# Three later passes over 768-token blocks instead of 512, with 384-wide quarter products and the second product two pairs later

## The chip, the cores and the metric

The kernel runs on one core of a Trainium2 chip. A core has TensorE (matrix products, PE in the profile; PEld is its loading of weights), VectorE (DVE), ScalarE (ACT), GpSimd (POOL), and SyncE (SP), which here issues the DMA transfers. Products are collected in PSUM, eight banks of 512 fp32 values on each of 128 partitions; everything else works on SBUF. The metric is device time in microseconds: 870.63 us before the change, the median of three runs from 869.15 to 870.75.

## What is computed

Retention on 4 sequences of 576 tokens with 8 heads of 64 (scores with a decay by distance, no softmax), and on its 2304 x 512 result two feed-forward layers with 2048 hidden features, everything in fp32:

```python
ret = scale * (q @ k.T) * decay          # decay 0 above the diagonal
x = (ret @ v).reshape(2304, 512)
h = x @ w_in                             # 512 -> 2048
x = (h * cos(h)) @ w_out                 # 2048 -> 512
h = x @ w2_in
out = (max(h, 0) + log1p(exp(-abs(h)))) @ w2_out
```

## The kernel before

Every fp32 product of the two layers is made of three products of fp32r parts: each operand is split into a rounded part (names with h) and the rest (names with l), and high by high, high by low and low by high are added. A copy on ScalarE makes the high part, a subtraction on VectorE (or GpSimd) the low part. The weights arrive as 64-bit numbers and are rebuilt by a few bit operations (`convert`, line 335).

The 2048 hidden features are 16 tiles of 128. The work on TensorE is in four passes. The first, `moe_a` (line 996), interleaves the retention with tiles 0 to 7 of the first layer, in five token groups of 512 and 384 with plain products; the half sum goes to DRAM (`pd`). The three later passes are `moe_c` (line 1154), each with four pairs of tiles: `ph` 0 has the rest of layer one, `ph` 1 and 2 the halves of layer two. They go over token blocks of 512, 512, 512, 512 and 256 (`CB`, `CO`), and for each block over the four pairs (`quad`, line 867).

A block of 512 tokens is two halves t of 256; the 512 input features are two halves d, the pair two tiles j. That is a 2 x 2 by 2 x 2 product of quarters, and `quad` makes it with seven products instead of eight (`PRODUCT`, line 864), of combinations of the weight quarters (made once a pass by `weight_pair`, line 434) and of token quarters (made for each block by `x_load_c`, line 1058, which also spills them to DRAM in `ph` 1, so that `ph` 2 only loads them). A product is six matmuls of 256 columns (two of depth 128, three parts each). The four results R1 to R4 come from a chain in PSUM: R1 and R4 lie in one bank, R2 and R3 in another, two pairs of banks (`ha` with `hb`, `s` with `o`) alternate. R1 is copied out (`cv`) after the first and again after the sixth product, R3's first part too (`c5`); VectorE adds these to R2 and R3 (line 932) and R4 = R1 + `c5` (line 935), and the seventh product ("4") is then added to R1. The 256-token block takes plain products, four of them, in one bank.

Then `activate` (line 785) works on each bank of 512: for layer one ScalarE, VectorE, VectorE or ScalarE, ScalarE (sine), VectorE, back into PSUM, for layer two VectorE, ScalarE, VectorE. It ends in the parts gh and gl, in two buffers each (`GB`). The second product takes these within the same pair's time, 24 matmuls of 512 columns: with tokens as columns in layer one, with tokens as weights and the 512 output features as columns in layer two. It is summed over the four pairs in `acc0` to `acc3`, and evicted at a block's end by an addition to the earlier half (`pt`, line 1186) and a store.

What runs when is not written by hand. `Plan` (line 117) takes every operation with an engine, an assumed duration, a due time and its dependences, and in `order` (line 147) puts at each step the operation that can start earliest on its engine, by the due time where two are equal. Constants at the top shift the due times: `XC` how far ahead a block's tokens are asked for, `W2` and `W3` the same for weights, `EARLY` and `EARLY_2` the copies and sums in `quad`. Operations marked "act or dve" or "pool or dve" get their engine there. The instructions are then issued in that order, and each engine runs its own in order.

Of the kernel before, what the change touches and what calls it, by code (L numbers as in the profile page):

```python
# [68 lines left out]
FLEX_AD = 1.075  # L69
FLEX_2 = 50.0  # L70
ROOM = 258.786
SPARE = 0.08
# [8 lines left out]
W2 = (34.03, 6.115, 14.31, 1.214)  # L81
W3 = (31.289, 12.304)
XC = 9.59
# [3 lines left out]
CA = (-3.373, 7.037, 4.372, 2.49)  # L87
TURN = 0.6
XS = 60.0
FILL = (2, 5)  # L90
EARLY = 1.692
EARLY_2 = 8.662
# [5 lines left out]
LL = 0.691  # L98
# [3 lines left out]
LEAD = 7.381  # L102
# [10 lines left out]
KQ = 0.903  # L113
QS = 3
# [136 lines left out]
def retention_moe_moe(ctx, tc, qkv, w1, w2, mask, mtail, dq, dk, out):  # L251
# [8 lines left out]
    xp = pool("xp", 1, side="right")  # L260
    pt = pool("pt", PT, side="right")
    wa_st = [ExitStack(), ExitStack()]
# [14 lines left out]
    sd = [dram.tile([128, len(CB), 7, 512], F32, name=f"sd{g}") for g in "hl"]  # L277
# [3 lines left out]
    mt_t = small.tile([128, 4, 64], F32, name="mt_t")  # L281
    dq_t = cst.tile([128, 4, 320], F32, name="dq_t")
    dk_t = small.tile([128, 12, 1], F32, name="dk_t")
    hp_t = small.tile([128, 1], F32, name="hp_t")
    T = {}
# [31 lines left out]
    UC = lambda n: 42 * t_mm(256) + 24 * t_mm(512) if n == 512 else 24 * t_mm(256) + 12 * t_mm(512)  # L317
    CM, t_ = [], MB
    for order in CO:
        CM.append([t_])  # L320
        for i in order:
            t_ += NP2 // 2 * UC(CB[i][1])
            CM[-1].append(t_)
# [110 lines left out]
    def weight_pair(layer, q, key, step, ahead):  # L434

        slot_ = q % (NP2 // 2)
# [3 lines left out]
        def make():  # L443
            p = wp["qqrp"[slot_]].tile([128, 5632], F32R, tag=f"pair{slot_}", name="pair")
            T[wk] = p[:, 0:1792], p[:, 1792:3584]
            T[wk, "o"] = p[:, 3584:5632].rearrange("p (j g d) -> p j g d", j=2, g=2)

        op("host", 0.0, key, make, r=[("qqrp"[slot_] + "open",)], w=[made], new=[(f"wp{slot_}", 1, wk)])
# [21 lines left out]
        for i, (x, y, o_, r) in enumerate((  # L470
                (lambda: Bv()[:, 0:256], lambda: Bv()[:, 256:512], ALU.add, [ak[1]]),
                (lambda: at(0), lambda: A()[:, 0:256], ALU.subtract, [ak[0], t_(0)]),
                (lambda: A()[:, 0:256], lambda: Bv()[:, 0:256], ALU.subtract, [*ak]),
                (lambda: A()[:, 256:512], lambda: at(1), ALU.subtract, [ak[0], t_(1)]))):
            def combine(e, x=x, y=y, o_=o_, i=i):
                if i % 2 == 0:
                    T[tt[i // 2]] = wp["q"].tile([128, 512], F32, tag="tt", name="tt", bufs=TT)
                e.tensor_tensor(at(i), x(), y(), o_)

            op(POOL_DVE, 256, k + 0.1 * i, combine, r=r + [("qopen",)], w=[t_(i)], new=[] if i % 2 else [("tt", TT, tt[i // 2])])  # L480
        for name, a in (("c", 3), ("d", 5)):
            split(name, a, a + 2, k + 0.6, lambda a=a: T[tt[a // 2 - 1]], [t_(a - 3), t_(a - 2)])
        if ahead:
            oks, ovs = load_values(layer, q, 1, key + 2 * step)
        for j in range(2):
            k = key + (2 + j) * step
            ok, ov = (oks[j], ovs[j]) if ahead else convert(layer, 2 * q + j, 1, k)
            op("act", t_act(512), k + 2.2, lambda j=j, ov=ov: nc.scalar.activation(T[wk, "o"][:, j, 0], ov(), AF.Copy),
               r=[ok, made], w=[(wk, "oh", j)])
            op(POOL_DVE, 512, k + 2.8, lambda e, j=j, ov=ov: sub(e, T[wk, "o"][:, j, 1], ov(), T[wk, "o"][:, j, 0]),  # L490
               r=[ok, (wk, "oh", j)], w=[(wk, "ol", j)])
# [118 lines left out]
    def masks(i, K):  # L610
# [19 lines left out]
        if c:  # L630
            d_k = (("dp", i),)

            def mask_tail():
                st["dp"] = small.tile([128, 64], F32, tag="dp", name="dp", bufs=3)
# [150 lines left out]
    def activate(layer, e, h_k, n, i, K1):  # L785
        kk, rk = ((g, "m", i) for g in ("ek", "er"))
        k_k, r_k = (kk,), (rk,)
        gh_k, gl_k = (("gh", i),), (("gl", i),)
        tmp = lambda g, dt=F32: ew.tile([128, n], dt, tag=g, name=g, padded_shape=[128, 512])
        H_ = lambda: e["h"][:, 0:n]  # L790
        if layer == 1:
# [18 lines left out]
            def a6():  # L810
                nc.vector.tensor_tensor(H_(), H_(), e["r"], ALU.mult)
# [5 lines left out]
            op("dve", t_dve(n), K1 + 2.3, a6, r=[r_k], w=h_k)  # L817
            K2 = K1 + 2.8
        else:
# [7 lines left out]
            def a7():  # L827
                nc.vector.scalar_tensor_tensor(H_(), H_(), 0.0, e["r"], ALU.max, ALU.add)
# [3 lines left out]
            op("dve", t_dve(n), K1 + 1.6, a7, r=[r_k], w=h_k)  # L832
            K2 = K1 + 2.8

        def g1():
            e["gh"] = gp.tile([128, n], F32R, tag="gh", name="gh", padded_shape=[128, 512])
            nc.scalar.activation(e["gh"], H_(), AF.Copy)

        def g2():
            e["gl"] = gp.tile([128, n], F32R, tag="gl", name="gl", padded_shape=[128, 512])  # L840
            sub(nc.vector, e["gl"], H_(), e["gh"])

        op("act", t_act(n, True), K2, g1, r=h_k, w=[gh_k], new=[("gh", GB, gh_k[0])])
        op("dve", t_dve(n), K2 + 0.5, g2, r=h_k + [gh_k], w=[gl_k], new=[("gl", GB, gl_k[0])])
# [20 lines left out]
    GROUP = "aabccdd"  # L865

    def quad(layer, q, xk, n, K, u, acc_id, acc, first, last):

        i = slots[0]
        slots[0] += 2
        wk = ("wp", layer, q)
        whole = n == 512
        tag_a, tag_b = (("ha", "hb"), ("s", "o"))[i // 2 % 2] if whole else (HT[i // 2 % 4], None)
        ka, kb = (tag_a, "q", i), (tag_b, "q", i)
        r1, r4, r2, r3 = (kb, 1), (kb, 4), (ka, 2), (ka, 3)
        ea, eb = {}, {}

        def banks():
            ea["h"] = bank(tag_a)
            eb["h"] = bank(tag_b) if whole else ea["h"]

        R1, R4 = (lambda z=z: eb["h"][:, z * 256:z * 256 + 256] for z in range(2))
        R2, R3 = (lambda z=z: ea["h"][:, z * 256:z * 256 + 256] for z in range(2))

        def product(out_, wi, xi, start, stop=True):
            y = 0
            for c in range(2):  # L890
                w_ = lambda g: T[wk][g][:, wi * 256 + c * 128:wi * 256 + c * 128 + 128]
                x_ = lambda g: T[xk][g][:, xi, c * 256:c * 256 + 256]
                for a, b in ((0, 0), (0, 1), (1, 0)):
                    nc.tensor.matmul(out_, w_(a), x_(b), start=(start and y == 0), stop=(stop and y == 5), skip_group_check=True)  # L894
                    y += 1

        def pe(todo, k, w, new=()):

            def run():
                if new:  # L900
                    banks()
                for o_, wi, xi, st in todo:
                    product(o_(), wi, xi, st)

            wi = sorted({GROUP[t[1]] for t in todo})
            op("pe", 6 * len(todo) * t_mm(256), k, run,
               r=[(wk, g, z) for g in "hl" for z in wi] + [(xk, g, t[2]) for g in "hl" for t in todo], w=w, new=list(new))

        new = [(tag_a, 1, ka), (tag_b, 1, kb)] if whole else [(tag_a, 1, ka)]
        if whole:  # L910
            P = lambda o_, z, st: (o_, *PRODUCT[z], st)
            ck, c5k = ("cv", i), ("c5", i)
            pe([P(R1, 1, True), P(R2, 2, True), P(R3, 5, True)], K, [r1, r2, r3], new)
            e = {}

            def copy_1(eng):
                e["cv"] = wp["q"].tile([128, 512], F32, tag="cv", name="cv", bufs=2)
                copy(eng, e["cv"][:, 0:256], R1())

            def copy_5(eng):  # L920
                e["c5"] = wp["q"].tile([128, 256], F32, tag="c5", name="c5", bufs=2)
                copy(eng, e["c5"], R3())

            def copy_6(eng):
                copy(eng, e["cv"][:, 256:512], R1())

            op(ACT_DVE, (t_act(256, True), t_dve(256)), K + 0.7 - EARLY, copy_1, r=[r1, ("qopen",)], w=[(ck, 0)], new=[("cv", 2, ck)])
            op(ACT_DVE, (t_act(256, True), t_dve(256)), K + 2.1 - EARLY, copy_5, r=[r3, ("qopen",)], w=[(c5k,)], new=[("c5", 2, c5k)])
            pe([P(R1, 6, False)], K + 0.9, [r1])
            pe([P(R3, 3, False)], K + 1.5, [r3])  # L930
            op(ACT_DVE, (t_act(256, True), t_dve(256)), K + 4.0 - EARLY, copy_6, r=[r1], w=[(ck, 1)])
            op("dve", t_dve(512), K + 4.5 - EARLY_2, lambda: nc.vector.tensor_tensor(ea["h"], ea["h"], e["cv"], ALU.add),
               r=[(ck, 0), (ck, 1)], w=[r2, r3])
            pe([P(R1, 7, False)], K + 2.0, [r1])
            op("dve", t_dve(256), K + 5.5 - EARLY, lambda: nc.vector.tensor_tensor(R4(), R1(), e["c5"], ALU.add), r=[r1, (c5k,)], w=[r4])  # L935
            pe([P(R1, 4, False)], K + 3.0, [r1])
        else:
            pe([(R2, 0, 0, True), (R2, 1, 1, False)], K, [r2], new)
            pe([(R3, 3, 0, True), (R3, 2, 2, False)], K + 1.0, [r3])
            both = activate(layer, ea, [r2, r3], 512, i, K + 0.5 * u)  # L940
        late = 0.0 if whole else LAG_S * u
        for j, (e_, hk, ready) in enumerate(((ea, [r2, r3], 0.45 * u), (eb, [r1, r4], 0.75 * u))):
# [332 lines left out]
```

## Time and profile before

| | |
|---|---|
| runs | 870.75, 870.63, 869.15 us, median 870.63 |
| the profiled execution: span | 871.2 us; no other time of it is given |
| TensorE busy | 857.9 us (98%), 5780 matmul instructions |
| weight loads busy | 753.3 us (86%) |
| VectorE busy | 647.2 us (74%) |
| ScalarE busy | 452.6 us (52%) |
| GpSimd busy | 47.3 us (5%), none after 300 us |
| DMA | 160.11 MB, mean 184 GB/s |
| chain that ended last | TensorE 92%, VectorE 3%, ScalarE, DMA and issue 1% each |

The span runs from the first to the last instruction of the profiled execution. Matmuls overlap in the array, so the listed duration of one (0.28 us for 256 columns, 0.39 for 512) is longer than the step from one to the next; the step is what a stream of them costs, and it is read from the chain of waits or from the starts in the timeline. The first quarter product (line 894) starts at 283.9 us; from there on the three later passes fill the rest.

### The profile page before, as it was taken

The numbers are of one execution on the slowest core, as the hardware profiler recorded it, in microseconds if no ns is written. First come the engines' busy times: TensorE is split into PE (matmuls) and PEld (weight loads), VectorE is DVE, ScalarE is ACT, GpSimd is POOL, SyncE is SP. The second block draws the span as 40 slices with busy tenths as digits, with TensorE's granted clock in tenths as the row PEclk, the third lists the DMA queues.
The fourth block names the chain that finished last, engine by engine and source line by source line (L and its number), as shares of the span: only waits on it lengthen the run. The fifth ranks groups of instructions, "written<-read, shape, count | busy, mean of one in ns | idle before, by whom it ended". The sixth has DMA issues, their size and how long they took to land.

```text
span 871.2 us, 15110 instructions
## 1 busy us (share of the span) xinstructions
PE 857.9 (98%) x5780; PEld 753.3 (86%) x5780; DVE 647.2 (74%) x1227; ACT 452.6 (52%) x873; POOL 47.3 (5%) x66
## 2 busy tenths in 40 slices
PE   7989999999999999999999999999999999999998
PEld 5768777899987889899898888998889888888897
DVE  3779987877479997578589997888568756465643
ACT  1368765756456855445458765655255533232221
POOL 3620100100030000000000000000000000000000
PEclk9989999999999999999999999999999999999999
DMA  9876779775363803245338469777525442432203
GB/s 312 319 267 187 275 250 340 259 271 173 131 229 97 254 22 101 64 144 166 110 117 283 146 252 316 225 252 311 217 92 190 165 170 97 169 97 73 97 2 108
DMA packets 67432, 160.11 MB, mean 184 GB/s; under 512 B 6048, under 2 KB 25632, under 8 KB 65312
## 3 DMA queue, kind: packets, MB, share of 16 engines
q1 hardware_dynamic: 67360, 159.15, 52.8%
q8 instruction: 45, 0.74, 0.4%
q14 instruction: 27, 0.22, 0.1%
HBM read 104.08 MB, written 55.05 MB: 183 GB/s over the span
## 4 chain that ended last, share of the span: by engine, by line
PE 92%; DVE 3%; ACT 1%; DMA 1%; issue 1%; SPq 0%; POOL 0%; DVEq 0%; POOLq 0%; ACTq 0%
PE acc L959 34%; PE acc L858 10%; PE o L894 9%; PE hb L894 9%; PE ha L894 7%; PE s L894 7%; PE ha L758 5%; PE hb L758 4%; PE o L671 2%; PE s L594 1%; PE o L758 1%; PE s L758 1%; PE s L599 1%; DMA dq_t<-in_dq 1%; DMA raw<-in_qkv 1%
## 5 line engine op out<-in xcount | busy, mean ns | idle before, releaser
L959 PE MATMUL acc<-pair,gh 128*128 128x512 f32 x576 | 179.3, 392 | 0.0
L959 PEld LDWEIGHTS acc<-pair,gh 128*128 128x128 f32 x576 | 101.3, 189 | 14.9
L959 PE MATMUL acc<-pair,gl 128*128 128x512 f32 x288 | 112.3, 390 | 0.0
L959 PE MATMUL acc<-gh,pair 128*128 128x512 f32 (+1 forms) x320 | 99.7, 370 | 0.0
L825 ACT ACTIVATE er<-er 128x512 f32<-128x512 f32 x72 | 45.5, 632 | 91.4 <-DVE er L822 91.4
L894 PE MATMUL o<-x,pair 128*128 128x256 f32 x328 | 78.3, 284 | 0.7 <-ACT cv L303 0.7
L894 PE MATMUL hb<-x,pair 128*128 128x256 f32 x328 | 78.8, 285 | 0.0
L894 PE MATMUL hb<-xx,pair 128*128 128x256 f32 x320 | 77.9, 285 | 0.0
L894 PE MATMUL o<-xx,pair 128*128 128x256 f32 x320 | 77.6, 285 | 0.0
L959 PEld LDWEIGHTS acc<-gh,pair 128*128 128x128 f32 x320 | 58.5, 189 | 8.6
L959 PEld LDWEIGHTS acc<-pair,gl 128*128 128x128 f32 x288 | 54.1, 188 | 11.8
L894 PEld LDWEIGHTS o<-x,pair 128*128 128x128 f32 x328 | 57.7, 189 | 5.1 <-DVE o L935 1.6
L894 PEld LDWEIGHTS hb<-x,pair 128*128 128x128 f32 x328 | 57.8, 189 | 4.9 <-DVE hb L935 2.4
L894 PEld LDWEIGHTS hb<-xx,pair 128*128 128x128 f32 x320 | 56.7, 189 | 5.0 <-DVE hb L935 2.1
L894 PEld LDWEIGHTS o<-xx,pair 128*128 128x128 f32 x320 | 56.6, 189 | 4.4 <-DVE o L935 2.1
L858 PE MATMUL acc<-gl,wh 128*128 128x512 f32 (+1 forms) x160 | 59.2, 370 | 1.2 <-DVE gl L299 1.2
L858 PE MATMUL acc<-gh,wh 128*128 128x512 f32 (+1 forms) x160 | 60.3, 377 | 0.0
L959 PE MATMUL acc<-gl,pair 128*128 128x512 f32 (+1 forms) x160 | 59.3, 371 | 0.0
L858 PE MATMUL acc<-gh,wl 128*128 128x512 f32 (+1 forms) x160 | 58.9, 368 | 0.0
L894 PE MATMUL ha<-x,pair 128*128 128x256 f32 x256 | 58.5, 283 | 0.0
L894 PE MATMUL s<-x,pair 128*128 128x256 f32 x256 | 58.5, 283 | 0.0
L808 ACT ACTIVATE er<-er,hp_t 128x512 f32<-128x512 f32 (+1 forms) x76 | 52.9, 697 | 10.5 <-DVE er L805 9.5
(196 smaller groups left out, 1999.8 us busy)
## 6 DMA issues: line engine op xcount, KB each, us to landing
wr<-in_w SPq DMA_DIRECT2D x64, 512.0 KB, 4.3
wd<-wk SPq DMA_DIRECT2D x40, 256.0 KB, 3.9
wr<-wd SPq DMA_DIRECT2D x20, 512.0 KB, 3.9
raw<-in_qkv SPq DMA_DIRECT2D x12, 640.0 KB, 5.4
raw<-in_qkv SPq DMA_DIRECT2D x12, 512.0 KB, 5.7
od<-pt SPq DMA_DIRECT2D x18, 256.0 KB, 2.4
pt<-od SPq DMA_DIRECT2D x18, 256.0 KB, 2.8
out<-pt SPq DMA_DIRECT2D x18, 256.0 KB, 2.0
```

Of the source, the lines that this page charges most:

```text
L594: nc.tensor.matmul(X()[j][:, z], k_(j, z), q_(z)[Z[j]], start=True, stop=True)
L599: nc.tensor.matmul(X()[0][Z[j], at_u(z)], kt_()[:, z, j], st["v"]()[:, z, j], start=True, stop=True)
L671: nc.tensor.matmul(o_at(z)[Z[j]], lhs(j), rhs(j), start=start, stop=stop, skip_group_check=True)
L758: nc.tensor.matmul(h_[:, 0:n], lhs, rhs[:, d, 0:n], start=(k == 0), stop=(k == 3 * NC - 1))
L808: nc.scalar.activation(e["r"], e["r"], AF.Sin, bias=hp_t[:, 0:1], scale=-1.0)
L825: nc.scalar.activation(e["r"], e["r"], AF.Softplus)
L858: nc.tensor.matmul(acc[o][:, 0:n], l[:, s], e[r], start=(first and z == 0), stop=(last and z == 2))
L894: nc.tensor.matmul(out_, w_(a), x_(b), start=(start and y == 0), stop=(stop and y == 5), skip_group_check=True)
L959: nc.tensor.matmul(acc[m][:, 0:n] if layer == 1 else acc[m], l, r, start=(begin and z == 0), stop=(stop and z == 2))
```

## The change

`CB` becomes three blocks of 768 tokens. A half block is 384 tokens, and all blocks take the seven products, now of 384 columns (`HN`). R1 to R4 have a bank each (`ha`, `hb`, `s`, `o`), so there is one set of four and not two of two. `activate` writes its last step to SBUF (`g`, three or four buffers for each half and tile), which frees the bank; gh and gl are made from there, still in two buffers, when the second product is due. That product is cut into units: `unit` does one half block t for one pair s, due in the time of pair 2 + 2t + s // 2, thus two pairs or more later and partly in the next block. Per unit there are 24 matmuls of 384 in `ph` 0, 18 of 512 in the others; the four `acc` banks hold one half block at a time. The token quarters lie in nine slots used in turn, so that the next block's can come while the last are in use. Weights for the second product have a tile of their own (`weight_out`). The jobs are given to the planner in order of due time, and its constants have new values. The first pass keeps its code; its last group's second products are due later (`LL`).

```diff
-CB = ((0, 512), (512, 512), (1024, 512), (1536, 512), (2048, 256))
-CO = ((0, 1, 4, 2, 3), (0, 1, 4, 2, 3), (0, 1, 2, 3, 4))
+HN = 384
+CB = tuple(range(0, NT, 2 * HN))
+NS = 9
...
-FLEX_AD = 1.075
+FLEX_AD = 0.993
-XC = 9.59
+XC = 9.717
-LL = 0.691
+LL = 3.862
+LAG = -2.133
+LEAD_G = 7.197
+GT = (3, 4)
...
+    DT = 6 * t_mm(HN)
+    IN, OUT = 7 * DT, (24 * t_mm(HN), 18 * t_mm(512))
+    UC = [IN + 2 * OUT[ph > 0] for ph in range(3)]
+    KI = lambda ph, y, s: CM[ph] + (half_p * y + s) * UC[ph]
...
-                nc.vector.scalar_tensor_tensor(H_(), H_(), 0.0, e["r"], ALU.max, ALU.add)
+                nc.vector.scalar_tensor_tensor(dst() if dst else H_(), H_(), 0.0, e["r"], ALU.max, ALU.add)
...
+    def quad(ph, y, s):
...
+        product(1, 1, K, True, True)
+        op(ACT_DVE, both, K + DT - EARLY, keep(1, 0, "v"), r=[rk[1], ("qopen",)], w=[(cv, 0)], new=[("cv", 2, cv)])
+        product(2, 2, K + DT, True, True)
+        product(3, 5, K + 2 * DT, True, True)
+        op("dve", t_dve(HN), K + 3 * DT - EARLY_2, lambda: nc.vector.tensor_tensor(R(2), R(2), c["v"][:, 0], ALU.add), r=[(cv, 0)], w=[rk[2]])
+        op(ACT_DVE, both, K + 3 * DT - EARLY, keep(3, 0, "5"), r=[rk[3], ("qopen",)], w=[(c5,)], new=[("c5", 2, c5)])
+        product(1, 6, K + 3 * DT)
+        op(ACT_DVE, both, K + 4 * DT - EARLY, keep(1, 1, "v"), r=[rk[1]], w=[(cv, 1)])
+        product(3, 3, K + 4 * DT)
+        product(1, 7, K + 5 * DT)
...
+        op("dve", t_dve(HN), K + 6 * DT - EARLY, fourth, r=[rk[1], (c5,)], w=[rk[4]], new=free(4))
+        op("dve", t_dve(HN), K + 5 * DT - EARLY_2, lambda: nc.vector.tensor_tensor(R(3), R(3), c["v"][:, 1], ALU.add), r=[(cv, 1)], w=[rk[3]])
+        product(1, 4, K + 6 * DT)
+        for r, j, t, ready in ((2, 0, 0, 3), (3, 0, 1, 6), (4, 1, 1, 6.5), (1, 1, 0, 7)):
...
+                    T[gk] = wp["r"].tile([128, HN], F32, tag=f"g{t}{j}", name="g", bufs=GT[t])
...
+    def unit(ph, y, t, s):
...
+        K = KI(ph, y, 2 + 2 * t + s // 2) + IN + (s % 2) * OUT[ph > 0] - LAG
...
+        for j in range(2):
...
+            Kj = K + j * OUT[ph > 0] / 2
+            rd = parts(e, lambda gk=gk: T[gk], [(gk,)], HN, i, Kj - LEAD_G, False)
+            for m in range(nm):
...
+                op("pe", OUT[ph > 0] / (2 * nm), Kj + 0.01 * m, mo, r=rd + [(wk, g, j) for g in "hl"], w=[(ak,)],
+                   new=[(tag, 1, ak)] if first else [])
...
+    XHOME = "qqqqrrrpp"
...
+            n = uses[0] % NS
+            uses[0] += 1
```

On TensorE, in the last pass, the end of one pair's quarter products before: hb holds R1 and R4, ha R2 and R3, x and xx are the token quarters' parts, pair the weights; the first piece is the product added before R4 is taken, the last six are the product behind it.

```order
L894 MATMUL hb<-x,pair 128x256
L894 MATMUL hb<-xx,pair 128x256
L894 MATMUL hb<-x,pair 128x256 x2
L894 MATMUL hb<-xx,pair 128x256
L894 MATMUL hb<-x,pair 128x256
L959 MATMUL acc_6495<-pair,gh 128x512 x2
L959 MATMUL acc_6495<-pair,gl 128x512
L894 MATMUL hb<-x,pair 128x256
L894 MATMUL hb<-xx,pair 128x256
L894 MATMUL hb<-x,pair 128x256 x2
L894 MATMUL hb<-xx,pair 128x256
L894 MATMUL hb<-x,pair 128x256
```

And now, where ha is R1, hb R2, s R3:

```order
L921 MATMUL hb<-x,pair 128x384 x6
L921 MATMUL s<-x,pair 128x384 x6
L921 MATMUL ha<-x,pair 128x384 x6
L921 MATMUL s<-x,pair 128x384 x6
L921 MATMUL ha<-x,pair 128x384 x6
L1001 MATMUL acc_6956<-pair,gh 128x512 x2
L1001 MATMUL acc_6956<-pair,gl 128x512
L1001 MATMUL acc_6963<-pair,gh 128x512 x2
L1001 MATMUL acc_6963<-pair,gl 128x512
L921 MATMUL ha<-x,pair 128x384 x6
L1001 MATMUL acc_6980<-pair,gh 128x512 x2
L1001 MATMUL acc_6980<-pair,gl 128x512
```

Six 512-wide matmuls of the second product stand now before the last product of a pair where three stood, and between the products on s, and on ha before, there are six of 384 where there were six of 256.

On VectorE, in the second pass, the making of gl among a block's preparation before: x and xx are token quarters (512 wide), tt their combinations, er and ha or hb the activation.

```order
L828 SCALAR_TENSOR_TENSOR hb<-hb,er 128x512
L371 SCALAR_TENSOR_TENSOR wk<-wy,wk 128x512
L299 TENSOR_TENSOR gl<-ha,gh 128x512
L299 TENSOR_TENSOR pair<-wr,pair 128x512
L299 TENSOR_TENSOR gl<-hb,gh 128x512
L299 TENSOR_TENSOR xx<-tt,x 128x512 x3
L1094 TENSOR_TENSOR tt<-xx,tt 128x512
L299 TENSOR_TENSOR xx<-xx,x 128x512
L932 TENSOR_TENSOR s<-s,cv 128x512
L935 TENSOR_TENSOR o<-o,c_5766 128x256
```

And now, with x and tt 768 wide and g the activated values in SBUF:

```order
L308 TENSOR_TENSOR x<-tt,x 128x768
L848 SCALAR_TENSOR_TENSOR g<-s,er 128x384
L308 TENSOR_TENSOR gl<-g,gh 128x384
L848 SCALAR_TENSOR_TENSOR g<-o,er 128x384
L308 TENSOR_TENSOR x<-tt,x 128x768
L308 TENSOR_TENSOR gl<-g,gh 128x384
L842 TENSOR_SCALAR er<-ha 128x384
L308 TENSOR_TENSOR x<-x 128x768
L848 SCALAR_TENSOR_TENSOR g<-ha,er 128x384
L308 TENSOR_TENSOR x<-tt,x 128x768
L308 TENSOR_TENSOR gl<-g,gh 128x384
L1175 TENSOR_TENSOR tt<-x,tt 128x768
```

The subtractions that make gl stood in pairs, one a half pair; now there are twice as many, each 384 wide, and single splits or combinations of 768 stand between them.

## Rows read from the trace of the kernel before

**Rows 1.** The page's first part: busy us, share of span, instructions.

```profile
PE 857.9 (98%) x5780; PEld 753.3 (86%) x5780; DVE 647.2 (74%) x1227; ACT 452.6 (52%) x873; POOL 47.3 (5%) x66
```

**Rows 2.** Busy time by stretch: stretch, length, each engine, TensorE clock, DMA share, GB/s.

```profile
283.90:478.00 194.10, 193.40 (x1258) 176.10 (x1257) 157.29 (x282) 116.38 (x217) 0.00 (x0) 1.00 0.43 139
478.00:672.00 194.00, 194.00 (x1215) 174.11 (x1214) 156.93 (x277) 108.86 (x208) 0.00 (x0) 1.00 0.62 220
672.00:867.10 195.10, 195.10 (x1204) 173.53 (x1202) 111.81 (x188) 61.33 (x115) 0.00 (x0) 1.00 0.31 114
867.10:871.20 4.10, 0.15 (x1) 0.00 (x0) 0.95 (x3) 0.00 (x0) 0.00 (x0) 0.78 0.35 128
```

**Rows 3.** Chain of waits, one pair of the last pass: start, us, what.

```profile
...
605.70 0.71 PE hb L894 x6
606.41 1.44 PE ha L894 x12
607.85 0.69 PE acc L959 x3
608.54 0.71 PE hb L894 x6
609.25 0.72 PE ha L894 x6
609.97 0.73 PE hb L894 x6
610.71 0.70 PE acc L959 x3
611.40 0.81 PE hb L894 x6
612.21 4.11 PE acc L959 x18
...
```

**Rows 4.** Chain of waits in the first pass, 384 and 512 wide.

```profile
...
185.79 2.08 PE ha L758 x12
...
265.01 2.72 PE ha L758 x12
...
```

**Rows 5.** Timeline within that pair: start, us, engine, line, operation, idle before it.

```profile
...
609.09 0.28 PE L894 MATMUL ha<-x,pair 128*128 128x256 f32 x1
609.29 0.38 ACT L303 ACTIVATE cv<-hb 128x256 f32<-128x256 f32 x1 [2.46 <-PE hb L894]
...
609.81 0.30 PE L894 MATMUL hb<-x,pair 128*128 128x256 f32 x1
...
610.42 0.28 PE L894 MATMUL hb<-x,pair 128*128 128x256 f32 x1
...
610.74 0.43 DVE L935 TENSOR_TENSOR hb<-hb,c 128x256 f32<-128x256 f32 x1
...
611.24 0.38 PE L894 MATMUL hb<-x,pair 128*128 128x256 f32 x1
611.45 0.28 PE L894 MATMUL hb<-xx,pair 128*128 128x256 f32 x1
...
```

**Rows 6.** Line 894: what its engine sat idle for (us, times).

```profile
...
  DVE hb L935: 4.5, 17
  DVE o L935: 3.8, 15
...
```

**Rows 7.** Groups by shape on VectorE and ScalarE: busy us, mean ns, idle before.

```profile
...
L299 DVE TENSOR_TENSOR gl<-hb,gh 128x384 fp32r<-128x384 f32 x6 | 3.3, 554 | 2.2 <-ACT gh L837 2.1
...
L303 ACT ACTIVATE pt<-acc 128x384 f32<-128x384 f32 x8 | 3.7, 493 | 0.1
L802 ACT ACTIVATE er<-er 128x384 f32<-128x384 f32 x6 | 3.1, 519 | 0.7 <-DVE er L798 0.6
...
```

**Rows 8.** Waits of TensorE from 200 to 300 us: total, times, longest.

```profile
...
PE acc L858 <- DVE gl L299: 0.6, 2, 0.5
```

**Rows 9.** The page's last part, DMA issues: KB each, us to landing.

```profile
...
wr<-wd SPq DMA_DIRECT2D x20, 512.0 KB, 3.9
...
```

More of the change, by code (lines that the diff above doesn't have):

```diff
@@ L284, in retention_moe_moe @@
     hp_t = small.tile([128, 1], F32, name="hp_t")
+    small.tile([128, PAD], F32, name="pad")
     T = {}
@@ L865, in retention_moe_moe @@
     GROUP = "aabccdd"
-    def quad(layer, q, xk, n, K, u, acc_id, acc, first, last):
+    xof = lambda ph, y, i: ("xc", ph, y, i)
+    gof = lambda ph, y, s, t, j: ("g", ph, y, s, t, j)
+    def quad(ph, y, s):
+        layer = 2 if ph else 1
+        q = s if ph == 1 else half_p + s
+        K = KI(ph, y, s)
         i = slots[0]
-        slots[0] += 2
+        slots[0] += 4
         wk = ("wp", layer, q)
[L875 to L897, printed above, removed]
@@ L899, in run, with product @@
+        tag = dict(zip((1, 2, 3, 4), HT))
+        key = {r: (tag[r], "q", i) for r in tag}
+        rk = {r: (key[r],) for r in tag}
+        e = {r: {} for r in tag}
+        R = lambda r: e[r]["h"][:, 0:HN]
+        cv, c5 = ("cv", i), ("c5", i)
+        free = lambda r: [(tag[r], 1, key[r])]
+        def product(r, z, k, start=False, new=False):
+            w_i, x_i = PRODUCT[z]
             def run():
                 if new:
-                    banks()
-                for o_, wi, xi, st in todo:
-                    product(o_(), wi, xi, st)
@@ L905, in pe @@
[L905 to L913, printed above, removed]
-            e = {}
[L916 to L940, printed above, removed]
@@ L941, in quad @@
[L941 to L955 removed]
+                    e[r]["h"] = bank(tag[r])
@@ new lines, in run @@
+                n = 0
+                for c in range(2):
+                    w_ = lambda g: T[wk][g][:, w_i * 256 + c * 128:w_i * 256 + c * 128 + 128]
+                    x_ = lambda g: T[xof(ph, y, x_i)][:, g, c * HN:c * HN + HN]
+                    for a, b in ((0, 0), (0, 1), (1, 0)):
+                        nc.tensor.matmul(R(r), w_(a), x_(b), start=(start and n == 0), stop=(n == 5), skip_group_check=True)
+                        n += 1
+            op("pe", DT, k, run, r=[(wk, g, GROUP[w_i]) for g in "hl"] + [(xof(ph, y, x_i), g) for g in "hl"], w=[rk[r]],
+               new=free(r) if new else [])
@@ new lines, in quad, with keep, run @@
+        both = (t_act(HN, True), t_dve(HN))
+        c = {}
+        def keep(r, z, name):
+            def run(eng):
+                if name == "5":
+                    c["5"] = wp["q"].tile([128, HN], F32, tag="c5", name="c5", bufs=2)
+                elif z == 0:
+                    c["v"] = wp["q"].tile([128, 2, HN], F32, tag="cv", name="cv", bufs=2)
+                copy(eng, c["5"] if name == "5" else c["v"][:, z], R(r))
+            return run
+        product(1, 1, K, True, True)
+        op(ACT_DVE, both, K + DT - EARLY, keep(1, 0, "v"), r=[rk[1], ("qopen",)], w=[(cv, 0)], new=[("cv", 2, cv)])
@@ L956, in mo @@
                     else:
[L957 removed]
+                        prods = [(l[:, z_], e[r]) for l, r in ((hi, "gh"), (hi, "gl"), (lo, "gh"))]
                     for z, (l, r) in enumerate(prods):
[L959 to L962 removed]
+                        nc.tensor.matmul(acc[m] if ph else acc[m][:, 0:HN], l, r, start=(first and z == 0), stop=(last and z == 2))
```

372 lines of the change are left out of this document (201 added, 171 removed).

## Prediction, made before the changed kernel was run

> **What bounds the kernel now.** I read the busy shares first: TensorE is busy for 857.9 us of the 871.2 us of the profiled span [rows 1]. The profiled execution has no time of its own apart from that span; the span is 0.6 us over the median of the timed runs (870.63 us), so I work on the span and take 0.6 us off at the end. Then the busy times by stretch. The change touches the three later passes, and these are the stretch from the first quarter product at 283.9 us to the last matmul at 867.1 us: 583.2 us, TensorE busy in practically all of it, at the full granted clock (2.4 GHz). VectorE is busy for 81% of the first two thirds (157.3 of 194.1 us and 156.9 of 194.0) and 57% of the last [rows 2]. So TensorE's stream sets the time, and VectorE is the engine to watch.
>
> Then the chain of waits, for the price of that stream. In an undisturbed part of the last pass one pair of hidden tiles on 512 tokens is nine pieces: 0.71, 1.44, 0.69, 0.71, 0.72, 0.73, 0.70, 0.81 and 4.11 us, 10.62 us in all [rows 3]. Twelve 256-wide matmuls take 1.44 us, 0.120 each; eighteen 512-wide ones 4.11 us, 0.2283 each. The 384-wide form is already in the first pass: twelve take 2.08 us, 0.1733 each, beside 2.72 us (0.2267) for 512 in the same code [rows 4]. From 256 to 512 a column costs 0.107/256 = 0.00042 us, so each matmul carries about 0.0133 us whatever its width; 384 lies on that line (0.1600 + 0.0133).
>
> Does it close? A pass has 4 blocks of 512 (16 pairs at 10.62 = 169.9 us) and one of 256 with plain products. The small block's pair is 24 matmuls of 256 and 12 of 512 in passes two and three (2.88 + 2.74 = 5.62, times 4 = 22.5), and 48 of 256 in pass one (5.76, times 4 = 23.0). That is 192.9 + 192.4 + 192.4 = 577.7 us, and with 24 matmuls that the first pass still has to do there (5.4 us) 583.1, against 583.2 measured. What the pieces are made of is thus all that there is, and no block start or pass start costs more than tenths.
>
> **The change part by part.** *Widths and counts.* Three blocks of 768, all with seven products, twelve pairs a pass. A pair has 42 matmuls of 384 (7.28 us) and a second product of 48 matmuls of 384 in pass one (8.32 us), 36 of 512 in the others (36 x 0.2283 = 8.22). Passes: 12 x 15.60 = 187.2 and twice 12 x 15.50 = 186.0; sum 559.2. Against 577.7 that is 18.5 us less. It has two sources. Matmuls alone: 2400 of 256 and 1248 of 512 become 2088 of 384 and 864 of 512, at the prices above 13.2 us less; 9,216 columns are 3.8 of it (the 256 block gets the saved product too) and 696 fixed parts of 0.0133 are 9.3. The other 5.3 us are waits inside the old pair, the next item.
>
> *The waits inside a pair.* In rows 3 the last six-matmul piece takes 0.81 us where its like take 0.71, and the one before 0.73. Rows 5 show why: the last product of a pair needs VectorE's sum, VectorE starts 0.20 us after the product before has been issued (610.54 to 610.74), takes 0.43, and TensorE goes on normally from 611.45, 0.09 us late; only three 512-wide matmuls (0.70 us) stand between. The copy by ScalarE goes the same way: its product has been issued at 609.09, where the next piece starts, the copy runs from 609.29 to 609.67, and the piece that waits for it starts at 609.81 with a first matmul 0.02 too long; 0.72 us stand between. All matmuls of that line show 8.3 us of idle time that the sums ended, 32 times, in the weight loads [rows 6]; most of that is hidden behind matmuls that still run. I take 0.11 us a pair, 48 pairs, 5.3 us.
>
> After the change the copies and sums are 384 wide: ScalarE 0.493, VectorE 0.554 us [rows 7]. With the same hand-overs (0.20 before, 0.16 behind) a copy needs 0.85 us and a sum 0.91. By the order, six 384-wide matmuls (1.04 us) or more stand between in every one of the 36 quads, and in passes two and three six 512-wide ones (1.37 us) before the last product. So these waits should go, by 0.13 to 0.46 us of slack, wherever the engine is free.
>
> *What is late next.* The activated values wait in SBUF, so the second product no longer hangs on the activation chain. But its operands gh and gl are made just before use, in two buffers, and one set now serves only 12 matmuls of 384 (2.08 us) or 9 of 512 (2.05 us) instead of 12 of 512 (2.74). A buffer's turn is: hand-over 0.20, ScalarE 0.52 (SBUF to SBUF [rows 7]), about 0.06, VectorE 0.554, hand-over 0.16; 1.5 us, an estimate from these rows. That leaves 0.5 us for whatever stands in front in VectorE's or ScalarE's queue. An operation of 384 just fits, one of 768 on VectorE does not: from 0.43 us for 256 [rows 5] and 0.554 for 384 I estimate 0.93 for it, so that the set would come 0.37 us late. The trace shows no such wait in the passes, since the old buffers had 2.74 us; bounds are 0 and, if each of the 96 sets of passes one and two met one operation of 768, 0.37 x 96 = 36 us. The nearest row is the old pair itself, which lost 0.11 us; I take 0.11 for each of the 36 new pairs, 4.0 us, and keep both ends.
>
> *VectorE and ScalarE in sum.* 144 activations of 384 take the place of 108 of 512, on the same columns. The 36 more are about three VectorE operations each with a fixed part of 0.18 us (0.554 less three steps of 0.124), 20 us; by the order 35 copies of 256 leave VectorE for ScalarE, 15 us. A few us over three passes, and at 81% that is covered by TensorE's stream: nothing in itself.
>
> *Rest of the edits.* Spilled operands are the same bytes in more transfers, asked for about 10 us ahead as before: nothing, hidden by the block before; if that cover failed, one landing of 3.9 us [rows 9] at each of 9 block starts, 35 us. Weights of the second product get their own slot and come later; their last use and next use lie two pairs (31 us) apart: nothing. The first pass ends with its second products later, so that two waits for gl (0.6 us [rows 8]) can go: -0.6. The tail is the same: two half-width sums of the last tile and its store behind the last matmul, 4.1 us [rows 2].
>
> Sum: 871.2 - 18.5 + 4.0 - 0.6 = 856.1 on the span, 855.5 as a run's time.
>
> **A rule against it.** The rows give each matmul 0.0133 us beside its columns [rows 3, 4]. The Trainium skill ("TensorE: Matmul & The Clock Gate", section "Back-to-back issue gap") gives a single matmul N/2.4 + 2.5 ns, which makes the fixed part five times smaller; by it the 696 matmuls fewer would be worth 1.7 us and not 9.3. The trace disagrees at all three widths (120, 173 and 227 ns, not 109, 163 and 216), so the sum goes by the rows; by the rule the time would be 1.7 us under that of the first rival.
>
> **Rivals.** *The fixed part stays.* If what I read as a cost of each matmul were a cost of each product or of the splits, only the columns (3.8), the balance of waits (5.3 - 4.0) and the 0.6 would be gained: 871.2 - 5.7 - 0.6 = 864.9 us. For it: the 256 rows and the 512 rows are different code. Against: 384 and 512 in one code lie on the same line. Chance 0.04.
>
> *Part is given back.* The buffers of gh and gl wait now and then: 0.05 to 0.1 us for each of 144 sets, 7 to 14 us in place of the 4.0: 858.7 to 865.7, middle 862. For it: VectorE's busy 81%, and the order, in which splits of 768 stand between two gl. Against: the slack of 0.5 us. Chance 0.25.
>
> *Slower.* The same place, but as a rule and not now and then: in passes one and two VectorE's queue is so mixed that each set comes late by 0.25 us, 96 x 0.25 = 24 us: 855.5 - 4.0 + 24 = 875.5. It decides from 19.1/96 = 0.20 us a set on. For it: each wait delays the activations behind it in the queue, which free the four product banks. Against: the old passes ran on that same share of VectorE, and their pieces close to 0.1 us without room for such waits. Chance 0.08.
>
> **Numbers.** My forecast has 0.63, with a range of its own of 851 (no new waits: 855.5 - 4.0 = 851.5) to 859. The range of 0.8: 850.5 to 864, which ends just under the first rival and takes in the given-back case but for its top. A measurement tells about 0.2% (1.7 us) from no change. Of the slower case's 0.08 I put 0.07 beyond that and 0.01 within it; 0.02 more within is a given-back case that goes further than priced. The rest, 0.90, is faster.
>
> **What would show it.** After: 2088 matmuls of 384 outside the first pass; a pair in the last pass of about 15.5 us in the chain, with no six-matmul piece longer than 1.06; passes of 186 to 190 us; and, in the list of waits, TensorE's on gl and gh of the second product below 5 us. The forecast is wrong if twelve 384-wide matmuls take over 2.1 us there, or if TensorE idles by more than 10 us between the first quarter product and the end; the window with the lowest TensorE share then says in which pass.

## The result, and the profile after

The changed kernel takes 858.48 us (median of 4 runs, 857.71 to 859.36) against 870.69 us for the kernel before (median of 4). The two medians give a ratio of 0.9860; the ratio on record is 0.9852, interval 0.9832 to 0.9873. In a second set of runs it was 0.9841 (0.9823 to 0.9859). The forecast of 855.5 us is 3 us low, inside its range and at the top of its own narrower one (851 to 859); the gain is 12 to 14 us where 15 were forecast.

The page of the changed kernel, busy time by engine and the chain by engine; it answers to [rows 1]:

```profile
PE 842.1 (98%) x5084; PEld 756.9 (88%) x5084; DVE 653.2 (76%) x1281; ACT 480.0 (56%) x951; POOL 53.2 (6%) x73
PE 86%; DVE 7%; ACT 3%; issue 1%; DMA 1%; SPq 0%; POOL 0%; DVEq 0%; POOLq 0%; ACTq 0%
```

TensorE has the 696 matmuls fewer and is as full as before. New is VectorE in the chain: 7% where it was 3%. Of its 63 us there 47 lie in the first pass and 14 in the first 80 us of the later passes; behind that the chain is TensorE's.

Its busy time by stretch, with columns as in [rows 2]; the first stretch begins at the first quarter product, the last is the tail:

```profile
278.06:470.00 191.94, 189.94 (x1074) 185.97 (x1073) 166.21 (x316) 133.03 (x261) 0.00 (x0) 1.00 0.41 139
470.00:661.00 191.00, 191.00 (x974) 174.65 (x973) 153.33 (x288) 111.63 (x215) 0.00 (x0) 1.00 0.61 218
661.00:851.90 190.90, 190.90 (x944) 170.75 (x942) 110.27 (x205) 70.58 (x142) 0.00 (x0) 1.00 0.33 114
851.90:855.90 4.00, 0.21 (x1) 0.00 (x0) 1.01 (x3) 0.00 (x0) 0.00 (x0) 0.78 0.53 197
```

Only the first stretch has idle time on TensorE (2.0 us). From the first quarter product to the last matmul there are 573.9 us; 36 matmuls of 512 belong to the first pass (36 x 0.2267 = 8.2), so the three passes take 565.7. The same reckoning on [rows 2] gives 583.2 - 5.4 = 577.8. The passes gained 12.1 us. A second execution of each kernel gives the same lengths: 565.7 and 577.8.

The chain of waits, one pair of the last pass (start, us, what); it answers to [rows 3]:

```profile
696.44 1.06 PE hb L921 x6
697.50 1.04 PE s L921 x6
698.54 1.04 PE ha L921 x6
699.58 1.04 PE s L921 x6
700.62 1.04 PE ha L921 x6
701.66 1.39 PE acc L1001 x6
703.05 1.04 PE ha L921 x6
704.10 4.80 PE acc L1001 x21
708.90 1.06 PE ha L921 x6
709.96 2.08 PE acc L1001 x9
```

A pair is 15.60 us (the next begins at 712.04); 15.61 was forecast (15.50 and 0.11). No wait is left in it. What is over the bare prices (42 x 0.1733 + 36 x 0.2267 = 15.44) lies where the width changes: the 512 pieces take 1.39, 4.80 and 2.08 us, not 1.36, 4.76 and 2.04, and two pieces of 384 behind them 1.06 and not 1.04. By the starts of the single matmuls it is up to 12 ns in each of the first five to nine behind a change.

Waits of TensorE in the passes (total, times, longest):

```profile
PE acc L1001 <- DVE gl L308: 1.1, 2, 0.8
PE s L921 <- DVE gl L308: 0.9, 1, 0.9
```

Both lie in pass one. The chain there (start, us, what):

```profile
279.88 0.70 DVE o L831
280.58 0.60 DVE gl L308
281.18 0.04 issue
281.23 1.33 PE s L921 x6
...
340.94 0.46 DVE pt L1034
341.40 0.48 DVE gl L308
341.87 0.04 issue
341.92 1.15 PE acc L1001 x5
...
```

At 281.23 the third quarter product has waited for bank s, which a gl of the first pass's last group was made from (VectorE works on the PSUM banks too, and ScalarE reads them): with one set of four banks the first quad needs all of them at once. At 341.92 the second product waits for gl behind the evictions (pt) at the start of the second block.

Groups by shape on VectorE, which answer to [rows 7] (busy us, mean ns, idle before):

```profile
L308 DVE TENSOR_TENSOR gl<-g,gh 128x384 fp32r<-128x384 f32 x144 | 79.6, 554 | 66.6 <-ACT gh L862 66.0
...
L308 DVE TENSOR_TENSOR x<-tt,x 128x768 fp32r<-128x768 f32 x24 | 22.7, 951 | 0.2 <-ACT x L1182 0.2
```

A 384-wide operation takes the 0.554 us assumed, a 768-wide one 0.951 (estimated at 0.93).

### The profile page after: what moved, and what is told of

It reads as the page before. It is cut to its first block, busy times and chain, and to the rows that moved or that the text cites. A ratio compares the mean times of both kernels' runs of the same rounds, so it can differ in the third digit from the quotient of the medians.

```text
span 855.9 us, 13829 instructions
## 1 busy us (share of the span) xinstructions
PE 842.1 (98%) x5084; PEld 756.9 (88%) x5084; DVE 653.2 (76%) x1281; ACT 480.0 (56%) x951; POOL 53.2 (6%) x73
## 4 chain that ended last, share of the span: by engine, by line
PE 86%; DVE 7%; ACT 3%; issue 1%; DMA 1%; SPq 0%; POOL 0%; DVEq 0%; POOLq 0%; ACTq 0%
PE acc L1001 34%; PE ha L921 17%; PE acc L883 9%; PE s L921 8%; PE hb L921 4%; PE ha L779 4%; PE hb L779 3%; PE o L692 2%; PE s L615 1%; DVE tt L1175 1%; DVE wk L382 1%; PE s L779 1%; PE s L620 1%; DMA dq_t<-in_dq 1%; DVE gl L308 1%
## 5 line engine op out<-in xcount | busy, mean ns | idle before, releaser
L921 PE MATMUL ha<-x,pair 128*128 128x384 f32 x864 | 174.3, 336 | 0.0
L921 PEld LDWEIGHTS ha<-x,pair 128*128 128x128 f32 x864 | 152.6, 188 | 5.1 <-DVE g L831 0.3
L308 DVE TENSOR_TENSOR gl<-g,gh 128x384 fp32r<-128x384 f32 x144 | 79.6, 554 | 66.6 <-ACT gh L862 66.0
L862 ACT ACTIVATE gh<-g 128x384 fp32r<-128x384 f32 x144 | 74.8, 521 | 92.1 <-PE acc L1001 88.4
L1001 PE MATMUL acc<-gh,pair 128*128 128x384 f32 x384 | 105.1, 334 | 0.0
L845 ACT ACTIVATE er<-er 128x384 f32<-128x384 f32 x96 | 50.3, 524 | 73.5 <-DVE er L842 73.0
L921 PE MATMUL s<-x,pair 128*128 128x384 f32 x432 | 86.8, 335 | 0.9 <-DVE gl L308 0.9
L921 PEld LDWEIGHTS s<-x,pair 128*128 128x128 f32 x432 | 75.9, 188 | 1.5 <-DVE gl L308 1.2
L1001 PE MATMUL acc<-gl,pair 128*128 128x384 f32 x192 | 64.5, 336 | 1.1 <-DVE gl L308 1.1
L828 ACT ACTIVATE er<-er,hp_t 128x384 f32<-128x384 f32 (+1 forms) x88 | 56.3, 643 | 15.5 <-DVE er L825 14.2
```

The source lines that it names most:

```text
L308: e.tensor_tensor(out_, a, hi.bitcast(F32), ALU.subtract)
L828: nc.scalar.activation(e["r"], e["r"], AF.Sin, bias=hp_t[:, 0:1], scale=-1.0)
L845: nc.scalar.activation(e["r"], e["r"], AF.Softplus)
L862: nc.scalar.activation(e["gh"], src(), AF.Copy)
L921: nc.tensor.matmul(R(r), w_(a), x_(b), start=(start and n == 0), stop=(n == 5), skip_group_check=True)
L1001: nc.tensor.matmul(acc[m] if ph else acc[m][:, 0:HN], l, r, start=(first and z == 0), stop=(last and z == 2))
```

## The experiments

Edits are against the changed kernel, unless the text says before. To compare with the changed kernel I set ratios beside its two, 0.9852 and 0.9841.

**The two kernels again.** Both unchanged.

> The kernel before once more, for its profile. If the part of the first pass ahead of 53 us (retention, TensorE waiting 2.9 us and then at the lower clock) differs between executions by chance, the first quarter product starts up to 2 us earlier than at 283.9 us here, and the span is nearer to the runs' median than 871.2. If the 3.1 us by which the first pass is shorter in the changed kernel come from the changed constants, it starts at 283.9 us again within 0.5.

> The changed kernel once more, on the chip of the other runs of this set, as what they are compared with: 858.5 us within 1, ratio to the kernel before 0.985. Pairs of passes two and three 15.60 us again.

The kernel before gave 872.77 us, with a span of 870.9; the changed kernel 858.25 us (857.54 to 859.41), spans 855.8 to 857.6. A run is thus 1.8 us longer than its span. Most of what differs between executions is the first pass: counted to the end of its matmuls, 289.3 and 289.1 us before, 286.2 and 287.9 after, and both kernels have code for it that differs little. The expectation's sign for the constants was seen: in the kernel before the first quarter product starts at 283.6 us, within 0.5 of 283.9. But in the changed kernel it starts at 279.7 us in this execution and at 278.1 in the first, with no constant changed. The granted clock of these executions shows much of why. First the kernel before, then the changed kernel, 20 to 60 us (the third column from the right is the clock):

```profile
20.00:40.00 20.00, 20.00 (x322) 15.40 (x321) 14.04 (x50) 6.49 (x20) 12.10 (x19) 0.93 0.95 365
40.00:60.00 20.00, 17.06 (x187) 13.63 (x184) 15.66 (x46) 11.06 (x31) 7.01 (x9) 0.83 0.74 255
```

```profile
20.00:40.00 20.00, 20.00 (x348) 15.55 (x342) 15.68 (x53) 5.97 (x19) 12.23 (x20) 1.00 0.93 368
40.00:60.00 20.00, 17.12 (x193) 13.42 (x189) 17.22 (x47) 14.36 (x36) 7.78 (x10) 0.91 0.82 273
```

The second execution of each, in the same order:

```profile
20.00:40.00 20.00, 20.00 (x316) 15.56 (x312) 13.74 (x49) 6.13 (x20) 12.11 (x20) 0.91 0.98 364
40.00:60.00 20.00, 17.02 (x200) 13.45 (x200) 17.04 (x49) 12.12 (x32) 7.36 (x9) 0.91 0.70 257
```

```profile
20.00:40.00 20.00, 20.00 (x316) 15.40 (x312) 13.62 (x49) 5.76 (x19) 12.09 (x20) 0.91 0.96 362
40.00:60.00 20.00, 17.48 (x206) 13.85 (x204) 17.09 (x49) 12.87 (x34) 7.80 (x10) 0.91 0.77 263
```

The means of 0.93, 0.83 and 0.91 are stretches at 1.2 GHz within 2.4, after TensorE had paused or been half idle (2.5 us without a matmul before 48.5 us in the changed kernel). Between the first two executions that is 20 x 0.07 + 20 x 0.08 = 3.0 us, against 3.1 between their first passes, and between the two of the changed kernel 1.8 against 1.7. But between the two of the kernel before it is 1.2 against 0.2, and between the second two nothing against 1.2, so this reckoning is good to about 1 us. Of the 15.3 us between the two profiled spans 12.1 are the change's passes, 0.1 the tail and 3.1 the first pass, most of that the clock; what the change itself takes from the first pass is 0.1 us by one pair of executions and 1.2 by the other. The medians (12.2 and 13.8 us apart) carry the 12.1 and at most 1.7 of first pass.

**More room before the last product, in the kernel before.** The planner is told that the sum for R4 takes 0.2 us longer, which puts six matmuls of 512 and not three ahead of a pair's last product.

```diff
-op("dve", t_dve(256), K + 5.5 - EARLY, lambda: ... R4() ...
+op("dve", t_dve(256) + 0.2, K + 5.5 - EARLY, lambda: ... R4() ...
```

> The kernel before, with the planner told that VectorE's sum for R4 takes 0.2 us longer, so that six 512-wide matmuls and not three stand ahead of a pair's last product. If the 0.10 us there are a wait for that sum, the pieces of 0.81 us become 0.72, a pair 10.52 us, and the run is about 4.6 us shorter (866.1). If they are only the cost of going from 512 to 256 columns, nothing changes (870.7). The order changes elsewhere too, by up to 1 us either way.

869.39 us, ratio 0.9965 (0.9952 to 0.9979), 3.1 us less. The chain in the last pass, where [rows 3] had 0.70, 0.81 and 4.11:

```profile
...
607.27 0.73 PE hb L894 x6
608.01 1.39 PE acc L959 x6
609.40 0.71 PE hb L894 x6
610.11 3.43 PE acc L959 x15
...
```

The piece of 0.81 is back at 0.71. It stood there in 33 of the old pairs (over 0.77 us; 33 x 0.10 = 3.3 us over their like), not in all 48, and stands in 3 here. So the mechanism is shown, and the old waits were worth about 3 us, not 5.3. In this version the passes are 2.3 us shorter, although a new wait at 445 us costs about 0.4.

**What a matmul costs beside its columns.** In pass three each quarter matmul is cut into 256 and 128 columns.

```diff
-nc.tensor.matmul(R(r), w_(a), x_(b), ...)
+for u, v in ((0, 256), (256, 384)):
+    nc.tensor.matmul(R(r)[:, u:v], w_(a), x_(b)[:, u:v], ...)
```

> The changed kernel with each 384-wide matmul of the quarter products of the last pass cut into one of 256 and one of 128 columns: 504 matmuls more, the same columns. If each matmul carries 0.0133 us beside its columns, a pair of that pass goes from 15.60 to 16.16 us and the run is 6.7 us longer (865.2). If a matmul carries 0.0025 us, 1.3 us longer (859.8). If the fixed part belongs to a product or to a switch between products, no change (858.5).

888.06 us, ratio 1.0179 (1.0161 to 1.0198): 29 us more, over four times what was expected. One pair of the last pass:

```profile
...
704.43 1.34 PE hb L923 x12
705.76 1.38 PE s L923 x12
707.15 1.39 PE ha L923 x12
...
```

Six of 256 and six of 128 take 1.34 to 1.39 us where six of 384 took 1.04. By the line through 256, 384 and 512 it would be 6 x (0.120 + 0.067) = 1.12 us. The starts show where the rest goes: a matmul of 128 is followed by the next one after 0.057 to 0.062 us, but one of 256 mostly only after 0.17, not 0.120. Every matmul here loads weights of its own, and the loads start one behind another, every 0.108 to 0.126 us, in this pass never closer than 0.108; two of them fill the 0.224 to 0.232 us of a 256 and a 128. There is a floor under the two matmuls together, so this run says nothing on the fixed part. The next expectation reads 0.111 us for 128 columns from the chain, which the starts don't bear out. The Trainium skill ("TensorE: Matmul & The Clock Gate", section "LDWEIGHTS (loading the stationary operand)") puts such a load at its columns over 1.2 in ns, 107 for 128; the 0.108 agrees with it. No run here took the load away, so that the load is the floor is read from these starts and was not tried.

So the second product of pass three was cut instead, each 512 into two of 256, above the floor.

```diff
-nc.tensor.matmul(acc[m] ..., l, r, ...)
+for u in (0, 256):
+    nc.tensor.matmul(acc[m][:, u:u + 256], l, r[:, u:u + 256], ...)
```

> The changed kernel with each 512-wide matmul of the second product of the last pass cut into two of 256, a width that the kernel before uses throughout: 432 matmuls more, the same columns. The cut to 128 columns before fell under a floor (0.111 us for 128 columns, read from its chain), which says nothing of wider ones. If each matmul of 256 or more carries 0.0133 us beside its columns, the run is 432 x 0.0133 = 5.7 us longer (864.0). If 256 columns, too, stand on a floor of the weight load and the parts of 0.0133 belong to something else, anything from 0 to 2.

863.26 us, ratio 0.9893 (0.9876 to 0.9909), 3.6 to 4.5 us over the changed kernel; its passes take 4.0 us more. The chain, parts of a pair:

```profile
...
752.67 1.04 PE ha L921 x6
753.71 5.03 PE acc L1003 x42
758.74 1.04 PE ha L921 x6
759.78 2.15 PE acc L1003 x18
...
```

A pair is 15.90 us: bare prices 42 x 0.1733 + 72 x 0.120 = 15.92. The 36 matmuls more cost 0.48 (0.0133 each), and the 0.16 for changes of width are gone: beside 256 the 384 pieces all take 1.04. Both together are the 0.30 seen. The fixed part of 0.0133 us holds. By the 2.5 ns that the Trainium skill ("TensorE: Matmul & The Clock Gate", section "Back-to-back issue gap") gives a single matmul beside its columns, 36 more would by estimate cost 0.09 us, less than the 0.16 that goes, and the pair would have become shorter.

**Three buffers for gh and gl.** `GB` 3; to have the room, `cv` and `c5` get one buffer each.

```diff
-GB = 2
+GB = 3
...
```

> The changed kernel with three buffers for gh and gl instead of two; to make room the kept copies cv and c5 have one buffer instead of two. If the waits on gl at the second block of pass one (about 335 and 341 us, 1.4 us in all) come from the turn of two buffers, they go, and the run is 1 to 2 us shorter (857). If they come from VectorE's order there, they stay, and nothing changes (858.3 within 0.7). Passes two and three stay at 15.60 us a pair under both.

859.18 us, ratio 0.9851 (0.9833 to 0.9868), the passes 565.6 us: nothing. TensorE's waits in the passes:

```profile
PE ha L921 <- ACT cv L312: 1.9, 1, 1.9
PE acc L1001 <- DVE gl L308: 0.8, 1, 0.8
```

The wait for gl at the second block stays, so it isn't for a buffer. The wait for `cv` took the place of the one for bank s; it is for the first copy of all, so no buffer was missing. The timeline shows what stood in front of that copy on ScalarE, while in the changed kernel the planner has the copy on VectorE:

```profile
...
282.04 2.29 ACT L1182 ACTIVATE x<-tt 128x768 fp32r<-128x768 f32 x3
...
284.24 0.47 ACT L312 ACTIVATE cv<-ha 128x384 f32<-128x384 f32 x1
...
```

The two gh and gl buffers are not what the passes lost to.

**The planner's constants.** `XC` asks for a block's tokens earlier, `LL` puts the first pass's last second products where they were before, `LAG` moves the units of the second product.

```diff
-XC = 9.717
+XC = 13.0
```

> The changed kernel with the tokens of each block asked for 13.0 us ahead and not 9.7. If the 1.07 us that TensorE loses at the third quarter product of pass one (281 us) are the preparation of the token quarters coming late on VectorE, the run is about 1 us shorter (857.3); the waits on gl at the second block may go or grow by as much. If they are the transfer, it also goes. Otherwise no change.

863.19 us, ratio 0.9898 (0.988 to 0.9915), some 4.5 us slower, against the expectation. The passes are 568.5 us, 2.8 more; in the first pass there is a new wait of 1.6 us for gl at 267 us. New in the passes are waits for copies:

```profile
PE ha L921 <- ACT cv L312: 1.8, 2, 1.2
PE s L921 <- ACT c L312: 1.3, 2, 0.7
```

At the first of them (283.8 us) splits of 768 stand ahead of the copy on ScalarE. That this holds for the others is how I read it; it was not tried by itself.

```diff
-LL = 3.862
+LL = 0.691
```

> The changed kernel with the last group of the first pass as before (LL 0.691). If the shorter first pass of the changed kernel's profile (3.1 us less than in the profile of before) came from that edit by the waits on gl that it took away, the run is 0.6 to 1 us longer (859); if it is mostly TensorE's clock around 40 to 60 us, which differs between executions, no more than that; if the edit made all of it, 3 us longer (861.3).

866.19 us, ratio 0.9932 (0.9918 to 0.9946), 7 to 8 us slower than the changed kernel and far more than expected. The passes take 570.4 us, 4.7 more; the rest lies in the first pass (288.4 us and not 286.2), where the waits on gl and gh are 2.0 us and not 1.0 and those for the first inputs 1.2 us longer. Most new waits of the passes lie in the first 70 us of pass one:

```profile
PE s L921 <- DVE g L831: 1.7, 1, 1.7
...
```

Half the gain thus hangs on one constant: with the first pass's last second products done early, TensorE reaches the second quad's bank s (300.7 us) before VectorE's activation has emptied it.

```diff
-LAG = -2.133
+LAG = 0.0
```

> The changed kernel with the units of the second product due 2.1 us earlier (LAG 0). By the order, TensorE's work in passes two and three then changes width twice a pair and not three times: the first quarter product of a pair stands beside the second and no longer alone among 512-wide matmuls. If what is left of a pair beside its matmuls (15.60 us against 7.28 + 8.16 = 15.44) is the change of width, some 0.05 us each way and back, a pair takes 15.54 to 15.56 and the two passes are 1.0 to 1.4 us shorter. If it is a wait, the pair stays at 15.60. Pass one, whose order moves too, can go either way by some us: the earlier changes of due times cost 3 to 8 us there.

> As e_lag0 with LAG -1: the same order in passes two and three, so the same 15.54 to 15.56 us a pair; pass one is ordered differently again. The difference between the two runs is then pass one and the first pass alone.

LAG 0: 861.44 us, ratio 0.9887 (0.987 to 0.9905); LAG -1: 861.08 us, ratio 0.9882 (0.9864 to 0.99). Pairs in passes two and three are 15.54 us, as expected, with the stream going from 384 to 512 and back twice a pair and not three times. Pass one, to the start of the 17th quad, takes 248.5 and 248.6 us. In the changed kernel it is 243.1, but nine 512-wide matmuls (2.0 us) that stand ahead of that quad here come behind it there; with them it is 245.2. So both versions are slower.

```diff
-LAG = -2.133
+LAG = 6.0
```

> The changed kernel with the units due 8.1 us earlier, half a pair (LAG 6), so that the second product follows its quarter products by one and a half pairs. If the lag of two pairs is what frees TensorE of waits, waits on gl, gh or the activated values come back in passes two and three and a pair gets longer than 15.60, by 0.1 to 1 us (861 to 880). If one and a half pairs are as good, the pairs stay within 0.05 of 15.60 and only pass one moves.

882.27 us, ratio 1.0117 (1.0102 to 1.0132): slower than the kernel before. The units come half a pair earlier, between the quarter products, and TensorE waits for VectorE and ScalarE:

```profile
PE acc L1001 <- ACT gh L862: 2.5, 1, 2.5
PE s L921 <- ACT c L312: 2.3, 4, 0.6
PE s L921 <- DVE c L314: 2.1, 3, 0.8
...
```

The passes lose 23 us beside the changed kernel's. About half of it comes before 480 us: TensorE falls 15 us behind its bare prices there, where the changed kernel falls 4, in steps of mostly 0.3 to 1.1 us on banks s, ha and hb. Some 6 us more follow by 540 us, and 2.6 in the wait for gh (2.5 in the list) at the last unit; the undisturbed pairs between take 15.71 us, 0.1 more than before the edit. The order of the units decides whether the copies and sums have room.

**Pass one's order with the others' short pairs.** `LAG` 0 for passes two and three alone.

```diff
-... + (s % 2) * OUT[ph > 0] - LAG
+... + (s % 2) * OUT[ph > 0] - (LAG if ph == 0 else 0.0)
```

> The changed kernel with LAG 0 instead of -2.133 in passes two and three only; pass one keeps its order on TensorE. Theory (the 0.06 us a pair that LAG 0 saved in passes two and three comes from one change between 384 and 512 columns fewer, and the 3.3 us that it lost came from pass one's order alone): pairs of 15.54 us in passes two and three, pass one as in the changed kernel (245.2 us from the first product to the 17th quad's start), the three passes 565.7 - 24 x 0.06 = 564.3 us, a run about 857 us, 1.4 us under the changed kernel, ratio to the kernel before 0.983 to 0.984. Rival (the loss of LAG 0 came from the lag itself, since each unit's weights and copies are then due at other times also in pass two): the passes 567 us or more, a run of 860 us or more.

856.59 us (855.88 to 858.26), ratio 0.9839 (0.982 to 0.9857); the passes 564.3 us, as expected to the tenth. A pair's end now:

```profile
...
638.41 1.39 PE acc L1001 x6
639.81 1.04 PE ha L921 x6
640.85 6.84 PE acc L1001 x30
...
```

It is the best version tried. The trace shows the 1.4 us; the ratios overlap with the changed kernel's and can't.

## Why the prediction was right, and where its terms were off

*The mechanism.* TensorE's stream set the time before and after, and counts times prices give the new one: 384 at 0.1733 us, 0.0133 us beside the columns (held by the cut second product), a pair of 15.60 us against 15.61. Passes two and three came out at 187.3 us each, with pairs of 15.60 us, once pass one's last units are done, but for three (15.65 to 15.75); the forecast for them was 187.3 (186.0 and 12 x 0.11). Pass one, at 191.1, lies outside the 186 to 190 that were to show the mechanism. There are 2088 matmuls of 384 (1512 for the quarters, 576 in pass one's second product). The rival in which the fixed part stays would have given 864.9 us and is out, and with it the 863.2 of the rule against the forecast.

*The waits inside the old pair* (5.3 us). The mechanism is right: more room before the last product took them away in the kernel before. The size is not: I took the 0.11 us of one pair for all 48, and 33 had it, 3.3 us. The term was also what was left of 18.5 after 13.2 for the matmuls, and that 13.2 goes by 0.2267 for 512; by the 0.2283 of the rest of the sum it is 13.8, which leaves 4.7. The 0.2283 already held a change of width (0.0016 over 0.2267), about 2 us in 1248 matmuls. That the sum of before closed so well was in part luck: 15 pairs without the wait are 1.5 us less, and 1.0 us that I had excluded came in at pass one's first block, where TensorE waits for the copy `cv` at 296.5 us.

*The waits in the new pair* (4.0 us allowed). In passes two and three the 0.11 a pair came out as 0.16, of which the 0.2283 held 0.06, but none of it is a wait; it is the width changing, as 15.54 us with one change fewer shows. Pass one lost about 3.9 us (565.7 less 2 x 187.3 is 191.1, against 12 x 15.60 = 187.2) where the allowance had 1.3, nearly all before 350 us. So "part is given back" happened in pass one, at about a third of its price (7 to 14 us; 0.1 x 144 is 14.4, so its top is 865.9 and not 865.7), and by another cause than that rival named: three buffers in place of two changed nothing. It is bank s at the first quad, and VectorE's and ScalarE's queues at the first two blocks.

*Together.* The passes were forecast at 559.2 + 4.0 = 563.2 us and took 565.7. That is 2.5 us: 2.6 in pass one, the rest nothing. On the side of before, 577.8 measured stand against 577.7. At the bare prices (0.120, 0.1733, 0.2267) the matmuls are 570.9 us before and 557.8 after, 13.1 less; beside them TensorE lost 6.9 us before and 8.0 after. So all of the gain is fewer matmuls and columns. The waits and changes of width, which I had as 1.3 us won (5.3 less 4.0), lost 1.1: the old waits went, and pass one's new ones and the changes between 384 and 512 cost more than those had.

*Slower.* It needs 0.20 us a set as a rule. The waits of the passes are 2.0 us in the list, three in all. A kernel slower than before is near all the same, by another way: with half a pair less lag (1.0117) TensorE waits mostly for the four banks and the copies and little for gl. My sum had no term for the choice of the lag.

*Rest of the edits.* I gave the first pass's later products 0.6 us; beyond the clock the first pass is 0.1 to 1.2 us shorter. Undone, they cost 7 to 8 us, 4.7 of them in the passes, because they then no longer stand between the first quads. The spill and the weights cost nothing that shows; `wr<-wd` lands in 4.5 us, 3.9 before [rows 9]. The tail is 4.0 against 4.1.

*From span to run.* I took 0.6 us off the span. A run is 1.8 us longer than its own span, in every run with both; the profiled execution of before was one with more time at 1.2 GHz in its first pass than the second. The forecast span of 856.1 would be 857.9 as a run, and with 2.5 more in the passes 860.4. The measured median lies 1.9 below that; the first passes traced ran to 286.2 and 287.9 us and not 289.3. So 3.0 us too low is 2.4 of conversion and 2.5 of pass one, less 1.9 of a quicker first pass. That the time fell within my own range of 851 to 859 is thus partly luck: the errors in pass one and in the conversion, 4.9 us together, would have taken it past the top.

## What to carry to other kernels

When one engine is full, price its stream by instruction count and width from the kernel's own rows, and check a repeated wait by counting how many repetitions show it before multiplying. A change that regroups work and moves it in time gains by the first and can lose it all by the second: where a later stage depends on copies and sums of other engines, look at the first block, when all buffers are still held by the stage before. A constant that only shifts an order can be worth as much as the change itself (7 and 24 us here), and different stages may want different values.

## What the runs showed of the hardware

- A stream that changes between 384 and 512 columns loses 0.02 to 0.04 us at most changes, in the matmuls behind it; between 384 and 256 no loss is seen.
- Matmuls of 256 and 128 columns in turn, each with a weight load of its own, cost 0.224 to 0.232 us for the two, where the line through the wider ones gives 0.187; the loads start 0.108 us apart at the least.
- The clock fell to 1.2 GHz for some microseconds after pauses of TensorE of 1.8 to 3 us, for longer in some executions than in others; after one pause of 2.0 us (changed kernel, 17.5 us) it did not fall. Two executions of the changed kernel have first passes of 286.2 and 287.9 us, with 0.91 in one and in two stretches of 20 us.
